# A searched priority table for the instruction order, and the queries of two head pairs transposed on VectorE, in a fused block-sparse attention and MoE kernel

## The chip, the cores and the metric

The kernel runs on one core of a Trainium2 chip. A core has five engines with their own in-order instruction queues: PE (TensorE, matrix products), DVE (VectorE), ACT (ScalarE), POOL (GpSimd) and SP (SyncE, which here only issues DMAs). The metric is the device time of one launch in microseconds (us), as the median over runs; lower is better.

## The reference, cut to what matters

```python
# q, k, v: (4, 8, 768, 64); block 64, 12 blocks, top_k 3
k_rep = k.reshape(B, H, n_blocks, block, D).mean(axis=3)
gate_scores = np.einsum('bhsd,bhnd->bhsn', q, k_rep)       # then causal by block
top_idx = np.argsort(gate_scores, axis=-1)[..., -top_k:]
# a query sees its own block and the 3 best earlier ones, causally
scores = scale * np.matmul(q, k.transpose(0, 1, 3, 2))
scores = np.where(mask & causal, scores, -1e9)
attn = softmax(scores)
x = np.matmul(attn, v)          # to (3072, 512)
h = x @ w_in                    # w_in (512, 2048)
g = 0.5 * h * (1.0 + np.tanh(c * (h + 0.044715 * h * h * h)))
out = g @ w_out                 # w_out (2048, 512), out (3072, 512) float32
```

Each query of a head chooses blocks of 64 keys by its product with the blocks' mean keys; attention runs over those blocks only; the result of all heads goes through a gelu layer of width 2048.

## The kernel before

Work is cut by batch (4) and by pair of heads (4 a batch, 16 pairs, numbered 0 to 15). For every pair `load` brings k, q and v by DMA from SP, `pre` transposes k and q so that the head dimension lies on the partitions, forms block means, computes the gates on PE (L517), and finds each query's blocks on VectorE (a 32x32 transpose at L540, then ten MAX8, compare, and combine: L547 to L561). The choice becomes additive mask rows, which PE adds to the scores as a further product or further rows. `heads2` (batch 0) and `heads` (batches 1 to 3) then run: score products into one of two PSUM buffers `wide`, an exponential on ScalarE (L705, L879) into one of six buffers `at`, POOL's triangle mask for diagonal blocks (L731, L893), the product with v (L754, L905), and the normalisation on VectorE. `turn_out` transposes the result to `xT`.

When a batch's attention is done, `s1` multiplies by `w_in` (L938, 128 matmuls of 384 columns a batch) and ScalarE applies gelu (L950) into `G`. For batch 0 the second product is plain (`s2_plain`, L1020, 96 matmuls of 512 columns). For batches 1 to 3 it is a seven-product scheme for 2x2 blocks (`s2`, L1070, 168 matmuls of 256 columns), which needs sums of weights (`w_sums`, L990, once, after the last plain product since one sum overwrites a part of w_out) and sums of gelu outputs (`sums`, L1008, 16 a batch), all on VectorE; VectorE also joins the results (L1115).

In batch 0 k and q are transposed by PE as fp32 products (L398, L401) and copied out of PSUM by VectorE or ScalarE; the scores of both heads share one product per key chunk, followed by a mask product over the same columns (L690). The loads of batch 0 land in memory that G and TS take later (`room`). From batch 1 on, k and q are loaded as blocks of 32x32 (rows of 128 bytes, L263) and VectorE transposes them (L418).

w_in is loaded by POOL (with a cast to fp16) once v of pair 3 has landed, w_out once k of pair 4 has; `hold` puts a tiny DMA on SP's queue (L326) that waits for w_in, and another for w_out, so that the loads of the batches behind them do not compete.

The order of instructions on each engine is not that of the program text. Each piece of work is an `Op` with its possible engines and a duration, its dependencies and a priority; `Plan.solve` runs a list schedule over modelled time, at each step taking the startable op with the lowest priority value, and emits everything in that order. The priorities are formulas, for example `1000 * b + 100 * hp` for a pair's attention. Matmuls that compute nothing (`warm`, L1168, 72 of them) have the worst priority and go where the planner finds PE without work. Most SBUF buffers come from tile pools, which hand out buffers in turn as instructions are emitted and add the waits that this needs.

Of the kernel before, what the change touches and what calls it, by code (L numbers as in the profile page):

```python
# [8 lines left out]
FP32 = mybir.dt.float32  # L9
# [8 lines left out]
SCALE = 0.125  # L18

# [113 lines left out]
def kernel(  # L133
# [13 lines left out]
    DM = H * D  # L147
# [8 lines left out]
    HALF = S // 2  # L156
    FAST = range(1, B)
    NCOLD = 18
    LAND = 3.0
    NWARM = 72  # L160
# [3 lines left out]
    io = ctx.enter_context(tc.tile_pool(name="io", bufs=PF))  # L164
    iov = ctx.enter_context(tc.tile_pool(name="iov", bufs=PV))
    hd = ctx.enter_context(tc.tile_pool(name="hd", bufs=3))
    hd2 = ctx.enter_context(tc.tile_pool(name="hd2", bufs=2))
    atp = ctx.enter_context(tc.tile_pool(name="atp", bufs=6))
    xtp = ctx.enter_context(tc.tile_pool(name="xtp", bufs=2))
    obp = ctx.enter_context(tc.tile_pool(name="obp", bufs=2))  # L170
# [17 lines left out]

    w_in16 = persist.tile([128, HP, DFF], FP16)
# [23 lines left out]
    for i in range(NB):  # L213
# [8 lines left out]
        "at": ([[x] for x in range(6)], 6), "osb": ([[x] for x in range(2)], 2),  # L222
# [20 lines left out]
    free_sd = {}  # L243

    def load(p, key, held=None, prio=None):
        b, hp = divmod(p, HP)

        def emit(_):
            sd = room.pop(0) if b == 0 and room else (
                iov if key == "v" else io).tile(  # L250
                [128, NC, 2, 64], FP32, tag=key, name=f"{key}_sd_{p}")
            for hh in range(2):
                nc.sync.dma_start(  # L253
                    out=sd[:, :, hh, :],
                    in_=SRC[key][b, 2 * hp + hh].rearrange(
                        "(c p) d -> p c d", p=128))
            T[key, p] = sd
        def emit_t(_):

            sd = io.tile([128, NC * 4, 32], FP32, tag=key, name=f"{key}_sd_{p}")  # L260
            for hh in range(2):
                for a in range(2):
# [5 lines left out]
        dve = key != "v" and p >= HP  # L268
        go = add({SP: 2.4 if dve else 1.15}, emit_t if dve else emit,
                 [free_sd.get((key, p - (PV if key == "v" else PF)))  # L270
                  if p - (PV if key == "v" else PF) >= HP else None, held]
                 + moved[-2:-1],
                 prio=10 * p if prio is None else prio)
# [25 lines left out]
    def cast_v(p, old):  # L299
        b, hp = divmod(p, HP)  # L300

        def emit(eng):
            copy(eng, v16[p % NB][:, :, :, 0:64], T["v", p])
        free_sd["v", p] = ld["v16", p] = add(
            {POOL: 0.85}, emit,
            [ld["v", p], old],
            prio=1000 * (b - 1) + 599 + hp if b else 100 * hp - 55)
# [74 lines left out]
    def pre(p):  # L382
# [5 lines left out]
        kcs, ksr, qcs = [], [], []  # L388
        ks = ks16[p % NK]
# [24 lines left out]
        def tr(key):  # L414
            def emit(_):
                T[key + "T32", p] = (hd if key == "q" else hd2).tile(
                    [128, S], FP32, tag=key + "T32", name=f"{key}T32_{p}")
# [5 lines left out]
        if first:  # L423
            for a in range(2):
                t = add({PE: 0.72}, turn("k", a),
                        [ld["k", p] if p else ld["k", 0, a]], pr,
                        takes=("pre", ("wk", p, a)))
                kc = add({DVE: 0.55},
# [3 lines left out]
                def ksb_h(_, a=a):  # L432
                    for x in ([ksb3[p % NK]] if p else
# [11 lines left out]
                        [t, last.get(p - NK, {}).get("gate")], pr - 0.1)  # L445
# [3 lines left out]
                if a == 1:  # L449
                    free_sd["k", p] = t  # L450
            T["ksb", p] = ksb3[p % NK]
        else:
            t = add({DVE: 0.98}, tr("k"),
                    [ld["k", p], last.get(p - 2, {}).get("k32"), sel_3[0]],
                    pr)
            free_sd["k", p] = t
# [6 lines left out]
            ksr.append(add({DVE: 0.93}, ks_all, [t], pr))  # L463
# [9 lines left out]
        def ksb_m(_):  # L473
# [7 lines left out]
                   ksr + [last.get(p - NK, {}).get("gate")], pr))  # L481

        last.setdefault(p, {})["k32"] = add({"NONE": 0.0}, lambda _: None,
                                            kcs + ksr, pr)

        if first:
            def q32():
                if ("qT32", p) not in T:
                    T["qT32", p] = hd.tile([128, S], FP32, tag="qT32",
                                           name=f"qT32_{p}")  # L490
                return T["qT32", p]
            for a in range(2):
                t = add({PE: 0.37}, turn("q", a),
                        [ld["q", p] if p else ld["q", 0, a]], pr,
                        takes=("pre", ("wq", p, a)))
                if a == 1:
                    free_sd["q", p] = t
                qcs.append(add({DVE: 0.55, ACT: 0.49}, turned("q", a, q32),
                               [t, last.get(p - 3, {}).get("pre")], pr,
                               gives=[("wq", p, a)]))  # L500
        else:
            t = add({DVE: 0.98}, tr("q"),
                    [ld["q", p], last.get(p - 3, {}).get("pre")], pr)
            free_sd["q", p] = t
# [4 lines left out]
        for a, (lo, hi) in enumerate(parts):  # L509
# [18 lines left out]
            last.setdefault(p, {})["gate"] = g  # L528

            def gm_e(_, a=a, lo=lo, hi=hi, n=n):  # L530
                if a == 0:
                    T["gx", p] = hd2.tile([128, NC - 1, 32], FP32, tag="gx",
                                          name=f"gx_{p}")
                    T["gm", p] = hd2.tile([128, NC - 1, 2, NBLK], FP32,
                                          tag="gm", name=f"gm_{p}")
                    T["mx8", p] = hd2.tile([128, NG, 8], FP32, tag="mx8",
                                           name=f"mx8_{p}")
                    T["sel", p] = hd2.tile([128, NG, NBLK], FP32, tag="sel",
                                           name=f"sel_{p}")
# [4 lines left out]
                     gives=[("gt", p, a)])  # L544

            def sel_e(_, a=a, lo=lo, hi=hi, n=n):
# [8 lines left out]
                for x in range(2 * lo, 2 * hi):  # L555
# [9 lines left out]
                      [gx, c_E["gates"], c_E["ones", i]], pr)  # L565
            sels.append(sel)

# [26 lines left out]
        def mask_dma(_):  # L594
            T["mT", p] = hd2.tile([128, S - 128], FP16, tag="mT",
                                 name=f"mT_{p}")
# [4 lines left out]
        if first:  # L601
            mcs = []
            for a, (lo, hi) in enumerate(parts):
                m = add({PE: 0.06 * (hi - lo)},
                        lambda _, a=a, lo=lo, hi=hi: mask(_, a, lo, hi),
                        [sels[a]], pr, takes=("pre", ("mk", p, a)))

# [652 lines left out]
```

## Time and profile before

| what | value |
|---|---|
| median of 8 runs | 265.11 us (264.97 to 265.71) |
| the profiled execution | 265.71 us |
| its span, first to last instruction | 264.0 us |
| busy: PE, DVE, ACT, POOL | 255.4, 180.8, 162.4, 82.9 us |
| granted TensorE clock | 0.999 |
| DMA | 32.63 MB, 127 GB/s of HBM over the span |
| chain that ended last, by engine | PE 58%, DVE 16%, SP's queue 10%, DMA 8% |

The profile is one execution on the chip. Busy time of PE includes matmuls that compute nothing, and ends of matmuls are modelled, so a busy PE is not a PE at its peak. A line such as "L705 ACT ACTIVATE at<-wide 128x1024 ... [0.62 <-PE wide L690]" in a timeline gives start, duration, line and engine, what was written from what, and in brackets how long the engine sat idle before it and what ended that. A row of a table by stage gives the stage and its length, then for PE, PEld (weight loads), DVE, ACT and POOL the busy time with the number of instructions, then granted clock, the DMA engines' busy share and GB/s.

### The profile page before, as it was taken

What the parts mean: (1) busy time and instruction counts of PE and PEld (TensorE: products, weight loads), DVE (VectorE), ACT (ScalarE), POOL (GpSimd) and SP (SyncE); (2) the same over time, 40 slices, a digit from 0 to 9 for tenths busy, and PEclk for the clock granted to TensorE, in tenths of its full rate; (3) what the DMA queues carried; (4) which work ended last, traced back from release to release, by engine and by line L of the source; (5) the groups of instructions that cost most, each with busy time, mean ns of one, the idle gap of its engine ahead of it and who ended that gap; (6) DMA issues with size and microseconds to landing.
All of it is one profiled execution on the core that took longest, in us unless ns stands there. A gap on an engine that the chain in (4) does not pass through costs nothing.

```text
span 264.0 us, 6523 instructions
## 1 busy us (share of the span) xinstructions
PE 255.4 (97%) x2542; PEld 177.3 (67%) x2542; DVE 180.8 (68%) x531; ACT 162.4 (62%) x203; POOL 82.9 (31%) x165
## 2 busy tenths in 40 slices
PE   6999999999998999999989999999999999999994
PEld 5777777565555555555756788655777797656883
DVE  1877744824389999989999999969644463335643
ACT  2268777566968886566887971367799912664000
POOL 8556734102346563221065743100044400000000
PEclk9999999999999999999999999999999999999999
DMA  8997899999798949888996962320104222000222
GB/s 161 219 206 150 135 211 124 178 203 192 146 200 161 220 109 220 170 168 140 158 189 124 163 152 81 104 52 0 27 1 122 52 79 83 0 0 4 79 80 81
DMA packets 130816, 32.63 MB, mean 124 GB/s; under 512 B 124544, under 2 KB 126688, under 8 KB 130784
## 3 DMA queue, kind: packets, MB, share of 16 engines
q1 hardware_dynamic: 126048, 27.62, 51.6%
q0 software_dynamic: 3136, 4.19, 9.9%
q10 hardware_dynamic: 1600, 0.39, 0.7%
q8 instruction: 20, 0.33, 0.5%
q14 instruction: 12, 0.10, 0.1%
HBM read 27.26 MB, written 6.29 MB: 127 GB/s over the span
## 4 chain that ended last, share of the span: by engine, by line
PE 58%; DVE 16%; SPq 10%; DMA 8%; issue 3%; POOL 2%; ACT 2%; DVEq 0%; ACTq 0%; POOLq 0%
PE bank L1070 19%; PE wide L938 16%; SPq L263 8%; PE wide L866 4%; DMA w_out<-in_moe_w_out_dram 4%; PE wide L690 4%; DMA q_sd<-in_q_dram 3%; PE bank L1168 3%; PE bank L905 3%; DVE XS L1008 2%; DVE qT L236 2%; PE bank L398 2%; SPq L253 2%; DVE qT L418 2%; DVE ks L459 2%
## 5 line engine op out<-in xcount | busy, mean ns | idle before, releaser
L938 PE MATMUL wide<-xT,w_in 128*128 128x384 f16 x512 | 85.1, 326 | 0.0
L950 ACT ACTIVATE G<-wide 128x768 f16<-128x768 f32 x64 | 51.8, 810 | 47.3 <-PE wide L938 47.3
L938 PEld LDWEIGHTS <-w_in 128*128 128x128 f16 x512 | 49.5, 98 | 33.2 <-issue 1.5
L879 ACT ACTIVATE at<-wide 128x896 f16<-128x896 f32 x72 | 61.3, 916 | 5.9 <-PE wide L866 4.4
L893 POOL TENSOR_SCALAR_AFFINE_SELECT at<-at 128x256 f16<-128x256 f16 x72 | 31.6, 441 | 68.5 <-ACT at L879 65.7
L866 PE MATMUL wide<-qT,kT 76*128 76x512 f16 (+1 forms) x192 | 38.6, 305 | 0.2
L1115 DVE TENSOR_TENSOR osb<-bank,osb 128x512 f32<-128x512 f32 (+1 forms) x36 | 22.3, 620 | 11.6 <-PE bank L1070 11.3
L1070 PEld LDWEIGHTS <-G 128*128 128x128 f16 x288 | 27.3, 98 | 4.2
L905 PEld LDWEIGHTS <-at 128*128 128x128 f16 x504 | 23.6, 97 | 9.2 <-POOL at L893 3.5
L1070 PE MATMUL bank<-w_out,G 128*128 128x256 f16 x216 | 29.6, 272 | 0.0
L905 PE MATMUL bank<-v,at 128*128 128x65 f16 x504 | 26.9, 194 | 1.1 <-DVE xn L794 0.6
L705 ACT ACTIVATE at<-wide 128x1024 f16<-128x1024 f32 (+3 forms) x24 | 21.4, 917 | 9.2 <-PE wide L690 8.0
L1020 PE MATMUL bank<-w_out,G 128*128 128x512 f16 x96 | 26.3, 379 | 0.6 <-DVE xn L794 0.6
L866 PEld LDWEIGHTS <-kT 76*128 76x128 f16 x192 | 15.9, 98 | 10.1 <-issue 1.4
L1070 PEld LDWEIGHTS <-XS 128*128 128x128 f16 x216 | 20.2, 98 | 3.6 <-DVE XS L1008 0.9
L1070 PE MATMUL bank<-TS,XS 128*128 128x256 f16 x144 | 20.3, 273 | 0.5 <-DVE XS L1008 0.5
L234 POOL CAST v<-v_sd 128x768 f16<-128x768 f32 x13 | 11.8, 907 | 25.3 <-DMA v_sd<-in_v_dram 25.2
L1008 DVE TENSOR_TENSOR XS<-G 128x768 f16<-128x768 f16 x12 | 6.6, 553 | 18.5 <-ACT G L950 18.5
L234 POOL CAST kT<-kT 64x768 f16<-64x768 f32 x17 | 13.9, 820 | 17.0 <-DVE kT L418 16.6
L418 DVE STREAM_TRANSPOSE kT<-k_sd 128x768 f32<-128x768 f32 x12 | 11.7, 972 | 6.1 <-DMA k_sd<-in_k_dram 6.0
L1168 PE MATMUL bank<-ident 128*128 128x256 f16 x72 | 13.1, 308 | 2.1 <-DVE ident L180 2.1
L794 DVE TENSOR_TENSOR xn<-bank,zr 128x384 f16<-128x384 f32 x24 | 13.4, 557 | 0.8
(96 smaller groups left out, 326.5 us busy)
## 6 DMA issues: line engine op xcount, KB each, us to landing
out_dram<-osb SPq DMA_DIRECT2D x24, 256.0 KB
v_sd<-in_v_dram SPq DMA_DIRECT2D x26, 192.0 KB
k_sd<-in_k_dram SPq DMA_DIRECT2D x48, 96.0 KB
q_sd<-in_q_dram SPq DMA_DIRECT2D x48, 96.0 KB
w_in<-in_moe_w_in_dram POOLq DMA_DIRECT2D x2, 1024.0 KB, 11.9
w_out<-in_moe_w_out_dram POOLq DMA_DIRECT2D x2, 1024.0 KB, 12.5
G<-in_k_dram SPq DMA_DIRECT2D x4, 192.0 KB
G<-in_q_dram SPq DMA_DIRECT2D x4, 192.0 KB
```

Of the source, the lines that this page charges most:

```text
L234: nc.gpsimd.tensor_copy(out=out, in_=in_)
L263: nc.sync.dma_start(out=sd[64 * hh + 32 * a:64 * hh + 32 * a + 32], in_=SRC[key][b, 2 * hp + hh].rearrange("(t i) (a j) -> a i t j", i=32, ...
L705: nc.scalar.activation(out=T["at", u][:, :, 0:n], in_=plan.buf[("st",) + u].rearrange("p (h w) -> p h w", h=2)[:, :, 0:n], func=AF.Exp, bi ...
L866: nc.tensor.matmul(st[:, x:e], kT16[i][h][0:76, s0:s0 + 128], qT16[i][h][0:76, s0 + (x - cb):s0 + (e - cb)], start=True, stop=True)
L879: nc.scalar.activation(out=T["at", u][:, 0:n], in_=plan.buf[("st",) + u][:, 0:n], func=AF.Exp, bias=0.0, scale=SCALE)
L893: nc.gpsimd.affine_select(out=dg, in_=dg, compare_op=ALU.is_ge, fill=0.0, base=0, pattern=[[0, 2], [1, 128]], channel_multiplier=-1)
L905: nc.tensor.matmul(pvv[:, qc, 0:65], at[:, cb + (qc - jc) * 128: cb + (qc - jc + 1) * 128], v16[i][:, jc, h, :], start=(gi == 0 and jc == ...
L938: nc.tensor.matmul(hps[:, 512 * e:512 * e + HALF], w_in16[:, ci, (2 * j + e) * 128: (2 * j + e + 1) * 128], T["xT", b][:, ci, HALF * h:HAL ...
L950: nc.scalar.activation(out=G[:, :, h, j, :], in_=plan.buf["hps", b, j, h].rearrange("p (e w) -> p e w", e=2)[:, :, 0:HALF], func=AF.Gelu_a ...
L1020: nc.tensor.matmul(plan.buf["ops", b, ti], G[:, f % 2, 2 * ti // NC, f // 2, ti % (NC // 2) * 128:ti % (NC // 2) * 128 + 128], w_out16[:, ...
L1070: nc.tensor.matmul(dst[:, HD * h:HD * h + HD], FACT[m][0][:, j, t * 128:(t + 1) * 128], FACT[m][1][:, j, :], start=(clear and j == 0), sto ...
L1115: nc.vector.tensor_tensor(out=dst(), in0=src(), in1=other(), op=ALU.add)
```

## The change

Five things are changed together.

- `RANK`, a table with one number for each op, replaces all priorities just before `solve`.
- `TURN` names the pairs of batch 0 whose queries are loaded in 32x32 blocks and transposed by VectorE, as in later batches: pairs 2 and 3.
- The buffers that tile pools handed out (loads, transposed k and q, selection scratch, `at`, `xn`, `zr`, `mT`, `osb`, `xT`) are named, and the planner assigns them as it does PSUM, with dependencies added where a pool's wait had been.
- In batch 0 the mask product leaves out queries for which the mask can't matter (the first 192, which have at most three blocks, and the first half of a diagonal chunk).
- Some of the planner's durations are changed.

```diff
+RANK = [
+    124, 118, 130, 122, 121, 123, 158, 223, 197, 39, 223, 67, 111, 224, 100,
...
+    1776, 1776, 1776, 1776, 1776, 1776]
...
+    TURN = {"k": (), "q": (2, 3), "v": ()}
...
-        "at": ([[x] for x in range(6)], 6), "osb": ([[x] for x in range(2)], 2),
+        **{kind: ([tuple(persist.tile([128] + dims, dt, name=f"{kind}_{n}_{m}")
+                         for m, (dims, dt) in enumerate(parts))
+                   for n in range(most)], most)
+           for kind, most, parts in (
+               ("at", 6, [([1024], FP16)]),
+               ("osb", 2, [([2, 2, HD], FP32)]),
+               ("ksd", PF, [([NC * 2 * 64], FP32)]),
+               ("qsd", PF, [([NC * 2 * 64], FP32)]),
+               ("vsd", PV, [([NC * 2 * 64], FP32)]),
+               ("k32", 2, [([S], FP32)]), ("q32", 3, [([S], FP32)]),
...
-        dve = key != "v" and p >= HP
+        dve = key != "v" and p >= HP or p in TURN[key]
...
-        if first:
+        if first and p not in TURN["q"]:
...
         else:
             t = add({DVE: 0.98}, tr("q"),
-                    [ld["q", p], last.get(p - 3, {}).get("pre")], pr)
-            free_sd["q", p] = t
+                    [ld["q", p]], pr, takes=("q32", ("q32", p)),
+                    gives=outside["q", p])
+            if b == 0:
+                early.append(t)
             qcs.append(t)
...
-                    for src, msk in ((kT2[i], False), (E2, True)):
-                        mov = mT2[i] if msk else qT2[i]
+                    q1 = max(q0, 192, jc * 128 + 64)
+                    for src, mov, lo in ((kT2[i], qT2[i], q0),
+                                         (E2, mT2[i], q1)):
+                        if lo >= q0 + w:
+                            continue
...
-            st = add({PE: n * 2 / 2400 + 0.01}, st_e, rdy[p][late], pr,
+            cols = n + sum(max(0, q0 + w - max(q0, 192, jc * 128 + 64))
+                           for jc, q0, w in unit)
+            st = add({PE: cols / 2400 + 0.1}, st_e, rdy[p][late], pr,
...
-                pvs[a].append(add({PE: 0.066 * len(cells) + 0.01}, pv_e,
+                pvs[a].append(add({PE: 0.06 * len(cells) + 0.1}, pv_e,
...
+        if b >= 2:
+            norms = norms + [gelus[b - 2][x] for x in gelus[b - 2]]
...
-            af = add({POOL: 0.36}, af_e, [ex], pr)
+            af = add({POOL: 0.44}, af_e, [ex], pr)
...
                 [mm, table(("gelu", b), exps[b], 1000 * b + 599)]
+                + (early if b == 0 else [])
...
+    assert len(RANK) == len(plan.ops)
+    for op, rank in zip(plan.ops, RANK):
+        op.prio = rank
     order = plan.solve()
```

`early` holds the ops of batch 0 that read its loads; the first gelus, whose output overwrites those loads, wait for them.

In the order that results, 40 of the 72 spare matmuls stand in batch 0's attention and its first product, four stand in the last batch's second product, and 28 behind the last product of all. ScalarE has the copies of 12 output pieces out of PSUM instead of 5, of 6 mask pieces of batch 1 instead of 3, and of 8 query halves instead of 10; VectorE has correspondingly 3, 2 and 16 instead of 10, 5 and 14; POOL has 19 key copies instead of 17 and VectorE 5 instead of 7.

## The prediction

> **What bounds the kernel now.** I read the page's engine shares first, then busy time by stage, then the spare matmuls alone in the same stages, then the timelines where PE wastes time. The stages are batch 0's attention (12.5 to 42.7 us of the span), batch 0's first MoE product (to 65.3), batch 1's attention mixed with batch 0's second product (to 95), a middle (to 157), and the rest.
>
> ```profile
> PE 255.4 (97%) x2542; PEld 177.3 (67%) x2542; DVE 180.8 (68%) x531; ACT 162.4 (62%) x203; POOL 82.9 (31%) x165
> ```
>
> PE looks like the bound everywhere. By stage (PE, PEld, DVE, ACT, POOL busy, count in brackets):
>
> ```profile
> 12.50:42.70 30.20, 30.14 (x475) 22.45 (x476) 19.99 (x79) 22.87 (x29) 15.89 (x28) 1.00 0.95 171
> 65.30:95.00 29.70, 28.62 (x293) 16.29 (x292) 23.29 (x71) 24.36 (x31) 14.88 (x27) 1.00 0.92 173
> 95.00:157.00 62.00, 60.46 (x598) 39.60 (x596) 60.06 (x154) 47.98 (x59) 25.35 (x44) 1.00 0.86 166
> 157.00:211.00 54.00, 54.00 (x549) 39.19 (x547) 37.23 (x119) 36.87 (x48) 13.00 (x28) 1.00 0.20 54
> 211.00:260.20 49.20, 49.12 (x395) 37.49 (x392) 22.62 (x42) 14.03 (x18) 0.04 (x1) 1.00 0.12 44
> ```
>
> Now the spare matmuls of L1168 alone, which compute nothing (PE, PEld):
>
> ```profile
> 12.50:42.70 30.20, 5.50 (x32) 2.63 (x33) 1.00 0.95 171
> 95.00:157.00 62.00, 1.69 (x14) 1.36 (x14) 1.00 0.86 166
> ```
>
> So PE is busy for show in two places. In batch 0's attention 32 spares fill holes; there the pace is set by ScalarE's exponentials waiting for scores:
>
> ```profile
> 15.04 1.94 ACT L705 ACTIVATE at<-wide 128x1024 f16<-128x1024 f32 x2 [0.62 <-PE wide L690]
> 18.91 1.73 ACT L705 ACTIVATE at<-wide 128x1024 f16<-128x1024 f32 x2 [1.94 <-PE wide L690]
> 20.52 0.87 ACT L232 COPY qT<-bank 128x384 f32<-128x384 f32 x2
> 28.31 0.48 ACT L232 COPY qT<-bank 128x384 f32<-128x384 f32 x1 [0.85 <-PE bank L401]
> 42.67 1.28 ACT L659 ACT_TABLE_LOAD   x1
> ```
>
> Two 1024-wide exponentials take 1.94 us, so about 0.92 each back to back; 19 of them, one of 768, one of 512 and three of 256 need 17.5 + 0.7 + 0.5 + 0.9 = 19.6 us, yet the stage lasts 30.1. In the middle VectorE is the bound (60.06 of 62.00 us), and PE runs 14 spares and then still waits for VectorE's sums of gelu outputs:
>
> ```profile
> 129.87 1.69 PE L1168 MATMUL bank<-ident 128*128 128x256 f16 x14
> 135.17 0.39 PE L1070 MATMUL bank<-TS,XS 128*128 128x256 f16 x2 [0.49 <-DVE XS L1008]
> ```
>
> From 157 to 260 PE is full of work that must be done. There only less work helps.
>
> **The change part by part.**
>
> *Queries of pairs 2 and 3.* Removed: 12 fp32 transposes on PE and four 128x384 copies out of PSUM. The chain shows six such transposes in 0.66 us, so 1.3 us of PE, in a stage where spares fill the holes: worth nothing by itself. The copies were 0.48 us on ScalarE or 0.56 on VectorE. Added: two VectorE transposes of 128x768.
>
> ```profile
> L418 DVE STREAM_TRANSPOSE qT<-q_sd 128x768 f32<-128x768 f32 x12 | 11.6, 963 | 0.0
> ```
>
> That is 2 x 0.96 = 1.9 us; VectorE is busy 19.99 of 30.20 us here, and all its rows of the stage, summed at the profile's means, go from 28.0 to 27.0 us, counted up to the end of this stage, because ScalarE takes two of pair 0's mask copies and the two VectorE copies go. In ScalarE's new order the four remaining query copies come before the first exponential, and nothing stands between the 24 exponentials. SP issues eight DMAs for the two loads instead of four (about 0.6 us each, hidden while DMA is full). The rows loaded are 128 bytes instead of 256:
>
> ```profile
> 8.00:13.00 5.00, 5.00 (x63) 3.94 (x63) 4.41 (x26) 0.95 (x2) 2.52 (x10) 1.00 1.35 218
> 74.00:77.00 3.00, 3.00 (x25) 1.63 (x24) 2.06 (x8) 1.02 (x2) 1.48 (x3) 1.00 1.09 174
> ```
>
> The first window moves only 256-byte rows (218 GB/s), the second almost only 128-byte ones (174). A load of 393 kB then takes 1.8 or 2.26 us: +0.9 us for both. The Trainium skill speaks against the change here: its page "DMA: Bandwidth & Descriptors", section Specifications, asks for at least 512 B per transfer for line rate. [...]if a row cost the same whatever its length, an estimate from that rule, the two loads would take twice 1.8 us more, +3.6. The trace does not show so steep a fall, so I take +0.9 and keep 3.6 as the upper end. What pays for it: pair 2's values now come behind pair 3's, so the load that releases w_in has one load fewer (1.8 us) ahead of it. On POOL w_in stands behind the same three masks of pair 1 as before, and its second half behind one more (0.41 us); I take its landing as unchanged, give or take 1 us.
>
> *Mask products only where a mask can matter.* Per pair 512 score columns lose the second product. The two heads run side by side; at 0.109 us per 256 columns (the spacing in L1070's long rows) that is 0.22 us x 4 = 0.9 us, again in the hole-filled stage: nothing by itself.
>
> *The table of priorities, stage of batch 0.* All other moves come from it. PE gets 11 spares between the first score product and the first MoE product instead of 30. The first exponential may be some 0.7 us later (PE does pair 1's query and key turns and both mask pieces first), but pair 0's six then run without a break, and pairs 1 to 3 are gated by VectorE's selection chain, whose rows sum to less than before. I estimate the last exponential at about 38.5 instead of 42.7: 4.0 us, just under half of the 10.5 us of slack. Bounds: -6 (pairs 2 and 3 wait only for their masks) and +1 (first exponential late, no wait gone). The next thing to be late would be w_in: its first half landed at 35.9 (SP's small DMA that waits for it starts then), so it allows this. The gain must then last: w_out's load is behind POOL's last triangle mask,
>
> ```profile
> 42.31 0.41 POOL L731 TENSOR_SCALAR_AFFINE_SELECT at<-at 128x256 f16<-128x256 f16 x1 [2.06 <-ACT at L705]
> 42.80 1.78 POOL L318 DMA_DIRECT2D w_out<-in_moe_w_out_dram  x2
> ```
>
> and behind pair 4's key load, so it moves up by 1 us at most, and batch 1's loads, which wait on SP for w_out, with it. What covers PE meanwhile is the second product of batch 0: 96 matmuls, some 20.5 us. If that cover is gone the 4 us are lost.
>
> *The table, middle.* Counting VectorE's instructions from pair 4's key transpose up to the first sum of the last gelu quarter of batch 1 (the sum chain that PE waited for at 135), at the rows' means, 77.3 us stood in the queue before and 66.6 us now: three 0.68 us output copies and three 0.49 us mask copies go to ScalarE, three 0.75 us key copies go to POOL or later, and pair 11's selection and query turn come later. So 10.7 us less before the sums. Against that, the last plain product of batch 0 now comes later, after 34 of batch 1's 128 first-product matmuls; the weight sums wait for it, and VectorE has 22.6 us of rows from the first weight sum to the last first-sum, PE 24.7 us of work in the same stretch (about 120 matmuls at 0.163, then scores and the unsummed product). The margin is 2.1 us. What can be won is what PE wastes: 1.69 of spares, 1.08 idle in 65.3-95 and 1.54 in 95-157, 4.3 in all. I take -3.2. Bounds: -6 (start-to-start gaps that the modelled ends hide) and +3.
>
> *Batches 2 and 3.* The same products in another mix; PE has no waste here, so zero at best. What covers each exponential is the second product of the batch before. I take 0 and keep +0.2 us for each of 48 exponentials as the bad end.
>
> *End.* 28 spares now follow the last product. The tenth waits for VectorE's last join (260.15 + 0.69); 19 at 0.109 and one ending of 0.27 bring PE to about 263.3, against SP's closing at 263.2. I take +0.1, bounds 0 and +0.4.
>
> *Explicit buffers and added dependencies* replace waits that pools made; no instruction is added. The one with work behind it is the first gelus' wait for every batch 0 load to have been consumed (their output lies over the loads): all ScalarE's gelus and the score buffers queue behind it. The last consumer is POOL's cast of pair 2's values, 0.87 us, which stands ahead of seven of POOL's triangle masks of this stage and so is long done. Zero; if that cast came last of all, 0.9.
>
> **Sum.** -4.0 - 3.2 + 0.1 = -7.1 us. The profiled execution took 265.71 us (span 264.0 plus 1.7); the median is 265.11, 0.6 lower. Taken from the median: 258.0 us.
>
> **The rivals.**
>
> *The data decide (about 262.2).* Batch 0's attention ends early, but w_out lands at 53 as before and pairs 5 to 7 come no sooner; PE runs out of cover and waits. Only the middle's gain stays: -3.2 + 0.1, and with a small loss to the slower query loads 262 to 264. For it: SP's queue, issuing loads, is 10% of the chain that ended last. Against: 20.5 us of cover.
>
> *ScalarE becomes the bound in batches 2 and 3 (slower, about 267.6).* An order fixed for modelled times meets the stretch where ScalarE has nothing to give:
>
> ```profile
> 195.00:210.00 15.00, 15.00 (x220) 11.79 (x219) 6.97 (x17) 15.00 (x20) 7.49 (x19) 1.00 0.30 75
> ```
>
> ScalarE takes on about 3 us of copies in all, and the mix of scores, PV and second products is no longer even: where PE's next instruction is a score product and both score buffers are held, all behind it waits. At 0.2 us for each of 48 exponentials it costs 9.6: 265.1 - 7.1 + 9.6 = 267.6. It decides from 0.15 us each, where 7.1 is used up. Against: outside 195-210 ScalarE is busy 36.87 of 54.00 us in that stage.
>
> *The table does nothing on the chip.* The planner's gain stays in the planner: 265.1.
>
> **How the numbers follow.** Forecast 0.42 (255.5 to 260.5), better than that with the bounds of both stages 0.08 (near 254), data decide 0.22 (260.5 to 264.6), nothing 0.03, ScalarE bound 0.25 (265.6 to 270). A measurement tells 0.2%, about 0.5 us, from no change. Faster 0.72, same 0.03, slower 0.25. The range 254 to 267 leaves out a few per cent below and about half of the ScalarE case above; the likeliest case's own range is 255.5 to 260.5.
>
> **What would show it.** Right: the gelu table load at 38 to 39 us, few spares between 12 and 130, no VectorE wait of PE at the first summed product of batch 1. Wrong: PE idle or spares before batch 1's scores (the data), or PE waiting on L879's successors between 157 and 215 (ScalarE). The forecast falls if the table load still comes at 42, or if w_in lands after 38.

## The result, and the profile after

The changed kernel takes 268.93 us (median of 11 runs, 267.09 to 270.3), beside 265.19 us for the kernel before in the same runs: a ratio of 1.0131, 95% interval 1.0112 to 1.015. It is slower by 3.7 us, where 258.0 was forecast and 267 was the upper end of the range. The profiled execution took 269.06 us, its span 267.4. Ratios leave out runs more than 1.5% above the fastest of their kernel, which concerns e2_before_late_q and e13_q4_256 below, so there a ratio is not the quotient of the medians.

First the engine shares and the clock row of the page of the kernel after, and the first line of its chain of waits:

```profile
PE 253.1 (95%) x2530; PEld 175.9 (66%) x2530; DVE 177.5 (66%) x519; ACT 167.0 (62%) x211; POOL 85.8 (32%) x167
PEclk9999999958999999999999999999999999999999
PE 84%; DMA 9%; SPq 3%; DVE 2%; ACT 1%; POOL 1%; issue 1%; DVEq 0%; ACTq 0%; POOLq 0%
```

PE has less to do than before and a longer span, so it stands still somewhere; the clock row says where (the 9th and 10th of 40 slices, 53 to 67 us). The stages around it (PE, PEld, DVE, ACT, POOL busy, granted clock, DMA share, GB/s):

```profile
45.00:50.00 5.00, 5.00 (x32) 2.92 (x30) 2.12 (x3) 3.24 (x4) 1.21 (x1) 1.00 1.18 164
50.00:55.00 5.00, 0.18 (x2) 0.00 (x0) 0.00 (x0) 0.00 (x0) 0.00 (x0) 0.72 1.42 214
55.00:60.00 5.00, 0.84 (x9) 0.33 (x10) 1.56 (x3) 0.93 (x2) 0.00 (x0) 0.50 1.01 181
60.00:65.00 5.00, 5.00 (x24) 2.66 (x23) 2.02 (x14) 2.22 (x3) 0.83 (x1) 0.75 0.98 165
```

From 50.2 to 58 us no engine computes and only the DMA engines work. Meanwhile the granted clock falls to 0.50, and the next matmuls go slowly until it is back. The timelines of VectorE, PE and ScalarE name what stood still:

```profile
58.06 0.98 DVE L585 STREAM_TRANSPOSE q<-qsd 128x768 f32<-128x768 f32 x1 [10.89 <-DMA qsd<-in_q_dram]
59.16 0.76 PE L693 MATMUL bank<-q,ksb 128*32 128x160 f32 x8 [8.98 <-DVE ksb L645]
59.07 0.83 ACT L391 CAST qT<-q 64x768 f16<-64x768 f32 x1 [9.34 <-DVE q L585]
```

In the kernel before the same transpose and the same gate product came without a wait:

```profile
47.85 0.96 DVE L418 STREAM_TRANSPOSE qT<-q_sd 128x768 f32<-128x768 f32 x1
50.55 0.48 PE L517 MATMUL bank<-qT,ksb 128*32 128x160 f32 x8
```

All three engines wait for one load, the queries of pair 4. PE's gate product for pair 4 stands in its queue after 36 of an unbroken row of the first MoE product, and nothing behind it may pass. In the chain of the kernel after this load is the longest wait; and these are the issues on SP, and on POOL the last mask of batch 0 and the issue of w_out:

```profile
44.02 13.96 DMA qsd<-in_q_dram
...
36.60 0.58 SPq L493 DMA_DIRECT2D held_in<-w_in  x1
37.22 5.04 SPq L427 DMA_DIRECT2D ksd<-in_k_dram  x4
42.31 2.24 SPq L427 DMA_DIRECT2D qsd<-in_q_dram  x4
...
39.14 0.41 POOL L911 TENSOR_SCALAR_AFFINE_SELECT at<-at 128x256 f16<-128x256 f16 x1 [0.51 <-ACT at L885]
42.67 0.19 POOL L482 COPY after_out<-ksd 1x16 f32<-1x16 f32 x1 [3.12 <-DMA ksd<-in_k_dram]
42.80 1.78 POOL L485 DMA_DIRECT2D w_out<-in_moe_w_out_dram  x2
```

In the kernel before the same rows read (its last mask and the issue of w_out stand in the prediction):

```profile
35.90 0.58 SPq L326 DMA_DIRECT2D held_in<-w_in  x1
36.52 4.36 SPq L263 DMA_DIRECT2D k_sd<-in_k_dram  x4
40.92 2.23 SPq L263 DMA_DIRECT2D q_sd<-in_q_dram  x4
...
42.67 0.19 POOL L315 COPY after_out<-k_sd 1x16 f32<-1x16 f32 x1
```

So the queries' load is issued 1.39 us later (0.70 because w_in's first half landed later, 0.68 because the key load's issue took longer), and w_out at 42.80 as before. The load's lead over w_out is 0.49 us instead of 1.88, and the two meet.

That w_out goes at 42.80 in both has two different causes. In the kernel before POOL was busy until then: its last mask waited for batch 0's last exponential and stood at 42.31, and the copy that waits for pair 4's keys found them landed (no wait in brackets). In the kernel after batch 0's attention ends sooner, the last mask is done at 39.55, and POOL waits 3.12 us for the keys. So the late mask had given the queries their lead, and the faster attention took it away: w_out now starts as soon as the keys are in. (No run moves the mask alone.) In the four profiles of the new order with this hold the lead is 0.49, 0.52 (e3_gate_late), 0.68 (e4_spares_in_wait) and 0.75 us (e13_q4_256), wherever between 41.61 and 42.31 the queries' load went out.

What the DMA queues moved from 47 to 56 us, q0 being w_out's queue and q1 SP's; first in the kernel after, then in the kernel before:

```profile
q0 software_dynamic: 1650, 1.67, 111.2%
q1 hardware_dynamic: 1543, 0.19, 27.8%
```

```profile
q0 software_dynamic: 1650, 1.67, 118.8%
q8 instruction: 1, 0.02, 0.7%
```

w_out moves at the same rate in both, 1650 packets in 9 us. In the kernel after nearly as many packets of SP's queue go through beside it, but they carry 128 bytes each where w_out's carry 1024, and 1543 in 9 us is 171 a microsecond. When w_out's packets began, from 45 to 47 us, SP's queue nearly stood still: 84 packets beside 205 of w_out. Alone they go much faster: in the kernel after, from 43 to 44 us, this queue moved 1422 of them.

```profile
q1 hardware_dynamic: 1422, 0.18, 110.8%
```

A load of 3072 such packets, 2.2 us at the rate it has alone (3072 by 1422), is thus landed only 14 us after its last DMA was issued.

### The profile page after: what moved, and what is told of

Its sections match the earlier page's. It is cut to its first block, busy times and chain, and to the rows that moved or that the text cites. A ratio compares the mean times of both kernels' runs of the same rounds, so it can differ in the third digit from the quotient of the medians.

```text
span 267.4 us, 6474 instructions
## 1 busy us (share of the span) xinstructions
PE 253.1 (95%) x2530; PEld 175.9 (66%) x2530; DVE 177.5 (66%) x519; ACT 167.0 (62%) x211; POOL 85.8 (32%) x167
## 4 chain that ended last, share of the span: by engine, by line
PE 84%; DMA 9%; SPq 3%; DVE 2%; ACT 1%; POOL 1%; issue 1%; DVEq 0%; ACTq 0%; POOLq 0%
PE wide L1124 28%; PE bank L1254 21%; PE wide L1049 10%; PE bank L1206 8%; PE bank L1088 6%; DMA qsd<-in_q_dram 5%; DMA w_in<-in_moe_w_in_dram 3%; PE bank L1351 3%; PE bank L693 3%; SPq L427 2%; PE wide L866 2%; PE bank L566 2%; ACT at L885 1%; PE bank L762 1%; PE bank L991 1%; PE bank L934 1%
## 5 line engine op out<-in xcount | busy, mean ns | idle before, releaser
L1124 PE MATMUL wide<-xT,w_in 128*128 128x384 f16 x512 | 90.0, 329 | 0.0
L1062 ACT ACTIVATE at<-wide 128x896 f16<-128x896 f32 x72 | 63.8, 917 | 10.5 <-PE wide L1049 6.8
L1049 PE MATMUL wide<-qT,kT 76*128 76x512 f16 (+3 forms) x192 | 38.6, 305 | 0.0
L1254 PE MATMUL bank<-w_out,G 128*128 128x256 f16 x216 | 31.1, 272 | 0.0
L393 POOL CAST kT<-k 64x768 f16<-64x768 f32 x19 | 17.1, 903 | 34.8 <-DVE k L585 34.2
L1088 PEld LDWEIGHTS <-at 128*128 128x128 f16 x504 | 22.0, 98 | 5.0 <-POOL at L1076 0.3
L1088 PE MATMUL bank<-v,at 128*128 128x65 f16 x504 | 24.1, 194 | 0.0
L585 DVE STREAM_TRANSPOSE q<-qsd 128x768 f32<-128x768 f32 x12 | 11.6, 968 | 10.9 <-DMA qsd<-in_q_dram 10.9
L693 PE MATMUL bank<-q,ksb 128*32 128x160 f32 (+1 forms) x128 | 7.8, 316 | 9.0 <-DVE ksb L645 9.0
L393 POOL CAST v<-vsd 128x768 f16<-128x768 f32 x13 | 11.5, 887 | 14.5 <-DMA vsd<-in_v_dram 13.8
```

The lines of the kernel that those rows point to most:

```text
L393: nc.gpsimd.tensor_copy(out=out, in_=in_)
L1049: nc.tensor.matmul(st[:, x:e], kT16[i][h][0:76, s0:s0 + 128], qT16[i][h][0:76, s0 + (x - cb):s0 + (e - cb)], start=True, stop=True)
L1062: nc.scalar.activation(out=T["at", u][:, 0:n], in_=plan.buf[("st",) + u][:, 0:n], func=AF.Exp, bias=0.0, scale=SCALE)
L1088: nc.tensor.matmul(pvv[:, qc, 0:65], at[:, cb + (qc - jc) * 128: cb + (qc - jc + 1) * 128], v16[i][:, jc, h, :], start=(gi == 0 and jc == ...
L1124: nc.tensor.matmul(hps[:, 512 * e:512 * e + HALF], w_in16[:, ci, (2 * j + e) * 128: (2 * j + e + 1) * 128], T["xT", b][:, ci, HALF * h:HAL ...
L1254: nc.tensor.matmul(dst[:, HD * h:HD * h + HD], FACT[m][0][:, j, t * 128:(t + 1) * 128], FACT[m][1][:, j, :], start=(clear and j == 0), sto ...
```

## The experiments

**e1_hold_q: w_out goes when pair 4's queries have landed.** One word; w_out then cannot meet that load, and the order of instructions stays the same on every queue.

```diff
-            [ld["k", HP]], 40, None if x else ("k", HP))
+            [ld["k", HP]], 40, None if x else ("q", HP))
```

> The changed kernel with one wait exchanged: POOL issues the load of w_out once the queries of pair 4 have landed, not their keys. Everything else, the order on every engine too, is the same. Theory A (the two halves of w_out take the DMA engines from the query load of pair 4, and PE stands behind it for 9 us): the query load lands within 3 us of its issue, PE's wait of 8.98 us at the gate of pair 4 goes, the granted clock is back to 0.99 or more, and the time is 258 to 261 us although w_out starts some 2 us later. Theory B (the query load is late for its own small rows, or the table's order is slow for other reasons): it lands after 50 as before and the time stays at 267 to 270. Theory C (w_out's later landing takes the wait's place): the wait at the gate goes, but PE waits for w_out or for batch 1's loads, 263 to 266 us.

259.06 us, beside 265.17 for the kernel before (0.9783, 0.9752 to 0.9813). In its timelines the queries are transposed at 46.66 without a wait, and PE goes through the gate without one:

```profile
49.28 0.48 PE L693 MATMUL bank<-q,ksb 128*32 128x160 f32 x8
49.69 6.51 PE L1124 MATMUL wide<-xT,w_in 128*128 128x384 f16 x39
```

The meeting of the two loads costs 268.93 - 259.06 = 9.9 us, and all else in the change gains 6.1. A second set of runs on another chip, beside the last experiments below, gave 257.68; by these the meeting costs 11.3 and all else gains 7.4.

> The kernel of e1_hold_q once more (259.06 us there), on one chip with the kernel without the trailing spares, since these two were run on different chips (ratios to the kernel before 0.9783 and 0.9723). Theory (the trailing spares cost nothing; the two differ by the chip): ratio 0.971 to 0.978, within 0.3% of the other. Rival (they cost 0.8 us or more at the end of the program): 0.4% or more above the other.

Ratio 0.9723 (0.9699 to 0.9746). This kernel beats both the kernel before and the kernel after.

**e8_before_hold_q: the same word in the kernel before.**

> The kernel before with the one edit of e1_hold_q: the small copy that holds w_out on the GpSimd queue reads pair 4's query tile instead of its key tile. Theory A (the edit has no gain of its own; it only takes the collision away, and the kernel before mostly has none): 264.8 to 266.5, w_out issued 0 to 2 us later than the 42.80 of the kernel before, no long wait anywhere between 42 and 60 us. Rival (the edit is a general gain, since the kernel before also loses time to the two loads sharing the DMA engines): 263 or less.

265.32 us beside 265.65 (0.9993, 0.9982 to 1.0004), w_out issued at 43.12. The edit alone is worth nothing; it only takes away a meeting that the kernel before does not have.

**e2_before_late_q and e9_before_late_q6: the meeting brought about in the kernel before.** SP issues three, or six, DMAs of 64 bytes ahead of pair 4's queries:

```diff
+            if key == "q" and p == HP:
+                for n in range(3):          # e9_before_late_q6: 6
+                    late = const.tile([1, 16], FP32, name=f"late_{n}")
+                    nc.sync.dma_start(out=late, in_=SRC["k"][b, n, 0:1, 0:16])
             sd = io.tile([128, NC * 4, 32], FP32, tag=key, name=f"{key}_sd_{p}")
```

> The kernel before with three tiny DMAs (64 bytes each) issued on SP just ahead of the query load of pair 4, so that it starts about 1.6 us later; nothing else is changed. Theory A: the query load now meets w_out as in the changed kernel, lands after 55 instead of before 46, PE stands 6 to 9 us at the gate of pair 4, which comes at 50.5, and the time is 271 to 276 us: the kernel before was less than 2 us away from this. Theory B: 1.6 us later, nothing else, 265 to 267 us.

The runs fell in two groups, 10 at 264.6 to 266.5 us and 10 at 270.9 to 273.4 (not 9, as the next expectation has it), and the ratio of 1.0008 (0.999 to 1.0025) covers the lower group only. The profiled execution was of that group: the three DMAs took only 0.97 us there, the load went out at 40.74, 1.21 us ahead of w_out (41.95), and VectorE waited 1.84 us for it. In nine of the ten longer runs the mean granted clock is 0.987 (0.994 in the tenth), as in most runs of the kernel after, and in the shorter ones 0.998 or more. That fits a long wait of PE, but no profile shows one of these runs.

> The kernel before with six DMAs of 64 bytes on SP's queue ahead of pair 4's query load, so that this load is issued about 3 to 4 us later than at 40.92 while w_out's issue at 42.80 stays. Theory A (what decides is whether the query load's packets are still on the DMA engines when w_out's packets start): now it meets w_out in every run, the query tile lands 8 us or more late, PE stands at pair 4's gate or at what is behind it, and the time is 270 to 275 in all runs, where with three such DMAs it was so in 9 of 20. Rival (the loss comes from the new order and not from the meeting of the two loads; a late issue alone costs its own 3 to 4 us at most and has 2 us of slack): 265 to 268.

276.56 us in the median of four runs, all above 274.6 (ratio 1.0417, 1.0358 to 1.0476), more than the 270 to 275 expected. The load went out at 41.80 and w_out at 42.47. The timelines of VectorE and PE, and the DMA queues from 50 to 52 us:

```profile
56.15 0.98 DVE L422 STREAM_TRANSPOSE qT<-q_sd 128x768 f32<-128x768 f32 x1 [8.56 <-DMA q_sd<-in_q_dram]
57.19 0.76 PE L521 MATMUL bank<-qT,ksb 128*32 128x160 f32 x8 [6.90 <-DVE qT L422]
...
q0 software_dynamic: 378, 0.38, 111.6%
q1 hardware_dynamic: 369, 0.05, 29.7%
```

The old order, old buffers and old priorities, with a lead of 0.67 us instead of 1.88, lose 11 us, nearly all in the same place: ScalarE's next table load comes at 74.63 instead of 65.93, 8.7 of the 8.9 us that the profiled execution lost. So the new order is not needed for the loss; a short time between the two issues is enough.

The two queues go one for one only in a part of this meeting. From 45 to 49 us w_out's queue moved 414 packets and SP's 174, from 50 to 53 it was 567 and 536, and from 53 to 56, when the load was nearly through, 603 and 117. What sets the share at the beginning and the end stays open.

**e13_q4_256: half as many packets for the same bytes.** In the kernel after, pair 4's queries alone are loaded in 256-byte rows, again with four DMAs, and are turned by PE; w_out keeps its old hold.

```diff
+            if (key, p) == ("q", HP):
...
+                        nc.sync.dma_start(
+                            out=T[key, p][:, 3 * a:3 * a + 3, hh, :],
+                            in_=SRC[key][b, 2 * hp + hh,
+                                         HALF * a:HALF * a + HALF]
+                            .rearrange("(c p) d -> p c d", p=128))
```

> The changed kernel (268.93 us), in which pair 4's query load alone reads 256-byte rows instead of 128-byte ones, with four DMAs as before, so half as many packets for the same bytes; PE then turns this pair's queries (six fp32 transposes into two free banks) and VectorE takes two copies out of them where its one transpose stood. w_out stays held behind the key load, so the two loads still meet. Theory A (from 47 us on the DMA engines take one packet of each queue in turn, so the small load's time is its number of packets left): in the changed kernel some 1,600 of 3,072 packets were left at 47 us and took 9 us to 56; now half as many are left and they land 4 to 5 us earlier, at about 53 to 54 instead of 58. PE's wait falls from 8.98 to 4 to 6 us (the turn through PE gives back about 1.3), and the time is 264 to 267.5. Rival B (the small load waits until w_out's bytes are through, or the two share by bytes): it lands at 56 to 58 as before, and with the turn's 1.3 us the time is 268.5 to 271.

266.78 us (263.98 to 269.3 over 20 runs; ratio 1.0044, 1.0023 to 1.0066). In the profiled execution, one of the shorter ones (264.37), the second half of the queries landed at about 51.4 and PE waited 2.62 us for it:

```profile
51.42 0.90 PE L600 MATMUL bank<-identk,qsd 128*128 128x128 f32 x3 [2.62 <-DMA qsd<-in_q_dram]
```

The queues from 48 to 50 us, of this kernel and then of the kernel after:

```profile
q0 software_dynamic: 310, 0.32, 94.0%
q1 hardware_dynamic: 285, 0.07, 27.5%
```

```profile
q0 software_dynamic: 370, 0.38, 111.6%
q1 hardware_dynamic: 366, 0.05, 29.5%
```

In each kernel the two queues take nearly as many packets as each other, while the bytes of the small load differ: 0.07 against 0.05 MB. In this stretch, then, the share goes by packets and not by bytes, and the larger rows get through sooner. The forecast landing was 53 to 54, and the load was earlier than that. It went out at 41.61 here, 0.75 us ahead of w_out instead of 0.49, and at 47 us 401 of its packets were left, 0.10 MB, where the kernel after still moved 1543, 0.19 MB, by 56. So a part of this gain is the lead and not the packet; the run does not separate the two.

**e3_gate_late: PE's gate moved behind 112 of 128 products.** Order alone, with the late load left in place.

```diff
+    gate = last[HP]["gate"][0]
+    to = order.index(s1_mm[0][13])
+    late = [gate]
...
+    order = ([o for o in order[:to + 1] if o not in late] + late
+             + order[to + 1:])
```

> The changed kernel with the gate of pair 4 and VectorE's selection behind it moved in the order: after 112 of the 128 first-product matmuls of batch 0 instead of after 36. The loads collide as before. Theory A with the cost in PE's order: the query load still lands at about 58, but PE works on meanwhile and reaches the gate at about 59: no wait of more than 1 us there, clock 0.99, time 259 to 263. Theory that the lateness of pair 4 itself costs the time: PE then lacks pair 4's scores after the first product and loses 5 us or more there, 265 to 269.

272.25 us (1.0259, 1.0228 to 1.0291): a miss, and slower than the kernel after. The timelines of PE and ScalarE, then two PE rows of later, when the pair's mask comes late:

```profile
60.32 2.08 PE L1124 MATMUL wide<-xT,w_in 128*128 128x384 f16 x6 [8.85 <-ACT G L1136]
58.73 0.83 ACT L391 CAST qT<-q 64x768 f16<-64x768 f32 x1 [9.01 <-DVE q L585]
...
74.94 0.39 PE L1206 MATMUL bank<-w_out,G 128*128 128x512 f16 x1
77.36 0.45 PE L762 MATMUL bank<-ident,madd 128*128 128x128 f16 x5 [2.03 <-DVE madd L730]
```

The expectation went by PE's queue alone. ScalarE's queue holds a cast of the same queries after six gelus; the gelus behind it keep both `wide` buffers, and PE is stopped after eight more products. Then the late mask costs another wait. A late load has to be looked for on every in-order queue.

**e4_spares_in_wait: the wait filled with matmuls that compute nothing.**

```diff
                 g = plan.buf["gt", p, a]
+                for _n in range(84 if p == HP else 0):
+                    nc.tensor.matmul(
+                        g[:, 0:256], ident16,
+                        ident16.unsqueeze(1).to_broadcast([128, 2, 128]),
+                        start=True, stop=True)
```

> The changed kernel with 84 spare matmuls of 256 columns (9.1 us at 0.109) put on PE just ahead of the gate of pair 4, where it stands for 9 us. If the clock's fall during the wait (granted 0.50 to 0.75 from 50 to 65) costs time, it is got back: the first product after the gate runs at 0.163 us a matmul from its start, clock 0.99, and the time falls by 1.5 to 2.5 us to 266.5 to 267.5. If the clock does not matter, the time stays at 269 (or rises by what the spares overrun the wait, under 1 us).

267.59 us (1.0092, 1.0073 to 1.0111), and the granted clock stays at 1.00 from 50 to 65 us:

```profile
50.09 9.33 PE L691 MATMUL bank<-ident 128*128 128x256 f16 x84
59.35 0.48 PE L698 MATMUL bank<-q,ksb 128*32 128x160 f32 x8
```

It is 1.3 us less than the kernel after. So of the 9.9 to 11.3 us about 1.3 are the clock's fall, and the rest is the wait and what it holds up.

**e7_hold_pe_turns: the queries of pairs 2 and 3 by PE again.** On e1_hold_q, with every other instruction in its place:

```diff
-        go = add({SP: 2.4 if dve else 1.15}, emit_t if dve else emit,
+        go = add({SP: 2.4 if dve else 1.15}, emit_t if dve and p >= HP else emit,
...
         def tr(key):
             def emit(_):
+                if p < HP:
+                    T["qT32", p] = plan.buf["q32", p][0]
+                    for a in range(2):
+                        w = T["bank", p][a]
...
+                            nc.tensor.transpose(
...
+                        nc.vector.tensor_copy(
```

> The changed kernel with w_out held behind pair 4's query load (the edit of e1_hold_q, 259.06 us), and in it the queries of pairs 2 and 3 turned by PE again: their loads read 256-byte rows with two DMAs each, and where VectorE's two transposes of 128x768 stand in the order, PE makes 12 fp32 transposes into two free banks and VectorE takes four copies of 128x384 out of them. Nothing else moves. Theory A (that part of the change is worth nothing by itself, as the prediction's sum had it; it costs or saves less than 1 us because batch 0's attention is filled with spares, and the two query loads are 0.9 us shorter on the DMA engines, so w_in lands up to 0.9 us earlier): 258.3 to 259.8, the gelu table load within 0.7 us of where it was (about 39 to 41), w_in issued up to 0.9 us earlier. Rival B (the turn by VectorE is what made batch 0's attention shorter): the table load comes 1.5 us or more later and the time is above 260.5. Rival C (the 128-byte rows of the two loads are what moved w_in, and so the loads behind it, late): w_in's issue back at 26.2 or less, and 258.0 or less.

260.36 us beside 265.65 (0.9809, 0.9783 to 0.9836), against 258.24 (0.9723, 0.9704 to 0.9742) on the same chip for the kernel of the next paragraph, which differs from e1_hold_q only in spares that prove to cost nothing. So rival B holds in kind and nearly in size: the turn by VectorE is worth 2.1 us here. The gelu table load comes at 43.31 instead of 40.86, and w_in goes out at 30.04, not earlier than the 27.44 of that kernel, so the row length of the two loads had not held it back (rival C). The rows of PE and VectorE show how; the last row is the same gate product in e10_hold_no_tail, the kernel that it is compared with:

```profile
22.50 0.87 PE L589 MATMUL bank<-identk,TS 128*128 128x128 f32 x6
23.08 1.02 DVE L593 COPY q<-bank 128x384 f32<-128x384 f32 x2 [1.25 <-PE bank L589]
24.16 0.48 PE L707 MATMUL bank<-q,ksb 128*32 128x160 f32 x8 [0.24 <-DVE q L593]
...
22.80 0.48 PE L693 MATMUL bank<-q,ksb 128*32 128x160 f32 x8
```

The copies out of PSUM take as long as a transpose (0.97 us), and PE's part lies ahead of them. The gate is 1.36 us later, of which 0.35 was there before these rows (the scores at 21.05 stand at 20.70 in the other kernel): some 1.0 us more for this pair on a chain that the next scores wait for, and about as much again for the next (2.45 us in all by the table load). The order is one made for VectorE's turn, so this is an upper end of what that part is worth.

**e10_hold_no_tail and e12_no_tail_again: e1_hold_q without the 28 matmuls after the last product.**

```diff
-    NWARM = 72
+    NWARM = 44
...
-    assert len(RANK) == len(plan.ops)
+    assert len(RANK) == len(plan.ops) + 28
```

> The changed kernel with w_out held behind pair 4's query load (e1_hold_q, 259.06 us), without the 28 spare matmuls that follow the last product. Theory (they run beside VectorE's last join and the last output DMA and end about when those do, as the prediction's +0.1 us had it): 258.6 to 259.2, no difference from e1_hold_q that can be told. Rival (they hold the clock's state or the end of the program): below 258.3, or above 259.8.

258.24 us, 0.8 below e1_hold_q's first runs, but on another chip; so the two were run again side by side.

> The kernel of e10_hold_no_tail once more (258.24 us there), beside the kernel of e1_hold_q. Theory (trailing spares cost nothing): the two agree within 0.3%. Rival: this one is 0.8 us or more faster, 257.5 to 258.5 against 258.8 to 259.8.

258.26 us (0.9731, 0.9708 to 0.9753) beside 257.68 for the kernel with the spares. They cost nothing that can be told.

**e5_formula_hold: all of e1_hold_q but the table.**

```diff
     for op, rank in zip(plan.ops, RANK):
-        op.prio = rank
+        pass
```

> The changed kernel with w_out held behind pair 4's query load, and with the priorities of the kernel's own formula instead of the searched table; all else of the change (queries of pairs 2 and 3 by VectorE, fewer mask products, explicit buffers, retuned costs) stays. Theory A (the table makes nearly all of the gain, as the prediction's sum had it): 263 to 266, within 2 us of the kernel before. Rival B (the other parts make half of the 6 us or more; the turn by VectorE alone was worth 1.3 to 2.1 us when it was undone in the table's order): 262.5 or less. Rival C (the formula's priorities do not fit the new costs): above 267.

262.60 us beside 265.13 (0.9903, 0.9883 to 0.9923), on the chip where the table's kernel took 257.68. The rest of the change gains 2.5 us and the table 4.9. The time lies between theory A (263 or more) and rival B (262.5 or less). The gelu table load is at 39.59 without the table as well, and 39.74 with it: what is gained in batch 0's attention comes without the table. From there to the end of the last product the formula's order takes 217.4 us (39.59 to 257.01) and the table's 212.0 (39.74 to 251.70): the table's gain lies behind the table load. The spare matmuls from 95 to 157 us (PE, PEld), of the kernel with the formula and then of e11_hold_q_again, show a part of it:

```profile
95.00:157.00 62.00, 2.89 (x22) 2.15 (x22) 1.00 0.90 168
```

```profile
95.00:157.00 62.00, 0.00 (x0) 0.00 (x0) 1.00 0.93 174
```

## Why the prediction was wrong, point by point

The sum was nearly right for a kernel that was not run: -7.1 us was forecast, and with the meeting of the loads taken away the change brings -6.1 (e1_hold_q) or -7.4 (e11_hold_q_again). That it comes so near is in part luck, since batch 0 gave less than its term and the rest more (below). What failed is a term that the sum did not have.

*The failed step* is the one on transfers: "The gain must then last: w_out's load is behind POOL's last triangle mask ... and behind pair 4's key load, so it moves up by 1 us at most". It asked whether w_out comes soon enough, and not what is on the DMA engines when it comes. It named both things that hold w_out, and did not ask which of them came last: it was the mask, and the change moves the mask. With POOL free at 39.55 w_out follows the keys at once, 0.49 us behind the issue of pair 4's queries, the one load that no hold covers. That costs 9.9 to 11.3 us. "I take its landing as unchanged, give or take 1 us" for w_in was right by its own bound (36.60 instead of 35.90), but 1 us was treated as a price, when a lead of 1.88 us was the whole distance to this loss. The +0.9 us for the query loads is not what moved w_in: POOL's copy that waits for pair 3's values starts without a wait in both kernels, behind a mask that begins at 26.73 instead of 25.70 because its exponential comes later. None of the three rivals was this one. The sign "PE idle or spares before batch 1's scores (the data)" did appear, with another cause, and the time lies 2 us above the range. That 268.93 falls into the range of the ScalarE rival (265.6 to 270) is chance, as its cause was not seen. The rule of the Trainium skill's page "DMA: Bandwidth & Descriptors", section Specifications (transfers of 512 B or more for line rate), which I weighed as +3.6 us for the two loads of pairs 2 and 3, does not explain the loss either: undoing those loads made the kernel slower, and the loss sits in a load whose row length the change left as it was.

*Batch 0's attention, -4.0.* The first six exponentials run nearly without a break, as forecast (no wait over 0.35 us once they have begun), and so do the last six (the last row of ScalarE's timeline before the table load):

```profile
35.04 5.24 ACT L885 ACTIVATE at<-wide 128x1024 f16<-128x1024 f32 x6 [0.17 <-PE wide L866]
40.72 1.28 ACT L832 ACT_TABLE_LOAD   x1
```

Between them waits remain: from 15.16 to 40.28 the exponentials take 25.1 us, where the prediction counts 19.6 us of work. The table load is at 40.72, or 39.7 to 39.9 in the two profiles of e1_hold_q's kernel, where 38.5 was forecast: -2.9 instead of -4.0 at best. Nor does it need the table, as the prediction had it (e5_formula_hold); it comes with the parts counted at "nothing by itself", of which only the turn was tested by itself, and not the mask products, the buffers or the durations. The turn by VectorE was one of them, costed at zero as PE filled its holes with spares; e7_hold_pe_turns puts up to 2.1 us on it. Spares show that PE has room, not that the chain through PE and back is short.

*Middle, -3.2.* First the spares alone in batch 0's attention and in the middle (PE, PEld), then the whole middle stage, all of the kernel after:

```profile
12.50:40.72 28.22, 2.70 (x13) 0.94 (x11) 1.00 0.94 169
...
95.00:157.00 62.00, 0.00 (x0) 0.00 (x0) 1.00 0.95 176
95.00:157.00 62.00, 61.96 (x616) 41.34 (x614) 59.63 (x163) 48.06 (x62) 28.41 (x47) 1.00 0.95 176
```

The 14 spares of the middle are gone, as forecast, with VectorE as full as before; batch 0 keeps 13 of 32. The time from the gelu table load to the end of the last product fell from 217.5 us (42.67 to 260.12) to 212.0 (39.74 to 251.70 in e11_hold_q_again): -5.5, more than the -3.2 taken and within the bound of -6. This stretch also holds batches 2 and 3, put at 0, and the runs do not split it; with the formula it takes 217.4, so the gain is the table's.

*Batches 2 and 3, 0* and the rival of a bound ScalarE: in the kernel after and in e11_hold_q_again PE is busy 54.00 of 54.00 us from 157 to 211, ScalarE 39.12 and 38.78, so that rival did not come about. *End, +0.1:* right, nothing that can be told. *The gelus' wait for all consumed loads, 0:* right; the first gelu follows the table load.

*The data decide (262.2; its own terms give 262.0)* expected w_out late for batch 0's second product. The data did decide, but through a load of 393 kB at 44 us.

## What to carry to other kernels

When a change shifts work by a microsecond, list for every large transfer which small loads are still on their way when its packets start, and how much time lies between the two issues; a small one caught then can take many times its own time (here 14 us, where 2.2 would do alone). Hold a large transfer behind the last load that must be ahead of it, not behind the last but one. Where two things hold it, look which comes last: a wait that never bound begins to bind when the change moves the other. A late load has to be followed on each in-order queue that has a reader of it (here VectorE, ScalarE and PE), since moving one reader away only shows the next.

## What the runs showed of the hardware that was not expected

- In the midst of such a meeting the DMA engines take about one packet of each queue in turn: 366 of 128 B beside 370 of 1024 B in 2 us, 369 beside 378 in the old order with the load made late, and 285 of 256 B beside 310. Alone, 1422 of the 128 B packets went in 1 us. In this part the small load advances by packets, not by bytes.
- It is not so throughout: in the first 2 us of w_out's packets the small load got 84 beside 205 (the kernel after, 45 to 47 us), and in e9_before_late_q6 117 beside 603 near its end (53 to 56 us). Why is open.
- In 9 us in which PE stood still the granted clock fell to 0.50, and the slow matmuls after it cost about 1.3 us; with the wait filled the clock stayed at 1.00 (e4_spares_in_wait).
- How sharp the edge is: with a lead of 1.88 us over w_out the queries' load costs nothing in the old order, nor with 1.21 in the profiled run of e2_before_late_q; with 0.67 it costs 11 us (e9_before_late_q6).
